# A second buffer for the x tile of the local heads, in an attention and mixture-of-experts kernel

## The chip, the cores and the metric

The kernel runs on one core of a Trainium2 chip. The metric is the time of one execution on the device in microseconds (us); of several runs the median counts. Engines: PE is TensorE (matmul), PEld its weight loads, DVE is VectorE, ACT is ScalarE, POOL is GpSimd, SP is SyncE; the last two issue DMAs here.

## What is computed

Attention over 4 batches, 8 heads, 576 positions and 64 numbers a head, then two feed-forward stages over the 2304 tokens. Four heads look at the 32 positions behind them (local), four at every 32nd position (strided):

```python
rel = pos[:, None] - pos[None, :]
mask_local = (rel >= 0) & (rel < 32)
mask_strided = (rel >= 0) & (pos[None, :] % 32 == pos[:, None] % 32)
attn = softmax(where(mask, q @ k.T / 8, -1e9))     # heads 0-3 local, 4-7 strided
x = (attn @ v) as [2304, 512]
e = argmax(x @ w_gate + modality_bias[modality_id]); x = gate * relu(x @ w1[e]) @ w2[e]
out = elu(x @ w_in) @ w_out
```

## The kernel before

`attention` (line 1072 on) goes over 16 pairs of heads, four for each batch b, in the order 2, 0, 3, 1: pairs 2 and 3 are strided, 0 and 1 local. So pair number n is strided where n is even and local where it is odd. The pairs are pipelined by a loop that is written out by hand; nothing reorders it. Iteration n makes the scores of pair n (`emit_S`: products on TensorE, mask L1274 and maximum L1277 on VectorE, subtraction L1278 on GpSimd), transposes q and k of pair n+1 (`emit_T`), transposes the weights of pair n-1 (`emit_PT`) and multiplies them by v (`emit_PV`), transposes the result of pair n-2 for the router (`emit_X`), then takes the exponential of pair n (`emit_exp`, L1283, on ScalarE between the two copies L1119 of `relay`), and loads q and k of pair n+3 and v of pair n+2 on SyncE's queue. Each engine works through its part in this order.

`emit_PV` ends with VectorE scaling the products, out of PSUM, into an x tile: L1336 for strided pairs, L1365 and L1368 for local ones. Two pairs share one x tile: one tile for the strided heads of a batch (`xs1`) and one for the local heads (`xs0`). The products come out of PSUM banks of the tag P, of which there are four; those of tag T, which the transposes of q and k and the router use, are two.

When the second pair of a tile is done, the stores of the tile to `x_dram` are put on the list `stores`: six for the strided tile (L1344), three for the local one (L1372, L1375). `store_x(3)`, called in `emit_S` right behind the subtraction on GpSimd, issues up to three of them on GpSimd's queue. With this order the six strided stores of a batch are issued three in iteration 4b+4 and three in 4b+5, and the three local ones in iteration 4b+6. In that same iteration `emit_PV` writes the first local pair of batch b+1.

From iteration 9 on a background generator (`early`) puts the routing of batches 0 and 1, the gathers from `x_dram` and the first expert's weights between these steps, one part per step of the loop. After the loop `ffn` runs: matrix products over the experts, then over w_in and w_out, with the rest of the attention (pair 15) threaded in.

Of the kernel before, what the change touches and what calls it, by code (L numbers as in the profile page):

```python
# [8 lines left out]
F32 = mybir.dt.float32  # L9
# [1062 lines left out]
def attention(tc, bg, q, k, v, mod, mbias, wg, x_dram, ident, router, bank):  # L1072
# [8 lines left out]
    xs_p = bctx.enter_context(tc.tile_pool(name="xs", bufs=1, side="right"))  # L1081
# [228 lines left out]
    xs, stores = {}, []  # L1310
# [3 lines left out]
    def emit_PV(n):  # L1314
        b, pr = pairs[n]
        strided = pr >= 2
        key = (b, pr // 2)
        h0 = 2 * (pr % 2)
        if key not in xs:
            sh = [128, 6, 4, D] if strided else [128, 18, D]  # L1320
            xs[key] = xs_p.tile(sh, F32, tag=f"xs{pr // 2}", bufs=1 + pr // 2, name="xs")
        x_sb = xs[key]
        xb = x_dram[b * S:(b + 1) * S]
        if strided:
            pss = [bank("P", "ps_v", 128, 6, D) for w in range(2)]
            for z in range(Z):
                for r in range(2):
                    for x in range(2):
                        for w in range(2):
                            ro = slice(64 * w, 64 * w + N3)  # L1330
                            at = (6 * r + 2 * z + x) * N3
                            nc.tensor.matmul(pss[w][64 * x:64 * x + 64, 2 * z + r], lhsT=pt_s[ro, at:at + 64],
                                             rhs=vs[pr - 2][ro, 3 * x + z, D * r:D * r + D], start=True, stop=True)
            rec = rss.pop(n)
            for w in range(2):
                nc.vector.tensor_tensor(x_sb[:, :, h0 + w], pss[w], rec[:, w].unsqueeze(2).to_broadcast([128, 6, D]), ALU.mult)  # L1336
                bg()
                bg()
            if pr % 2:
                o = xb[:, 4 * D:].rearrange("(j c) d -> j c d", c=32)  # L1340
                for y in range(6):
                    i, x = divmod(y, 2)
                    cnt = min(6, 32 - 6 * y)
                    stores.append(lambda y=y, cnt=cnt, at=64 * x + J * i: nc.gpsimd.dma_start(  # L1344
                        o[:, 6 * y:6 * y + cnt], x_sb[at:at + J, 0:cnt].rearrange("j s h d -> j s (h d)")))
            return
        parts = [(0, TAIL + 1), (TAIL + 1, 9)]
        pss = [bank("P", f"ps_v{r}", 128, j - i, D + 1) for r, (i, j) in enumerate(parts)]
        for r in range(2):
            for s in range(4):  # L1350
                for x in range(2):
                    nc.tensor.matmul(pss[r][64 * x:64 * x + 64, s], lhsT=pt_l[:, parts[r][0] + s, 64 * x:64 * x + 64],
                                     rhs=vl[pr][:, 2 * s + x, r], start=True, stop=True)
        for r in range(2):
            nc.tensor.matmul(pss[0][64 * r:64 * r + 64, TAIL], lhsT=pt_l[:, TAIL, 64 * r:64 * r + 64],
                             rhs=vl[pr][:, 8, r], start=True, stop=True)
        rs = m_p.tile([128, 9], F32, tag="rs", name="rs")
        for ps, (i, j) in zip(pss, parts):
            nc.vector.tensor_scalar(rs[:, i:j], ps[:, :, D], 1e-9, None, ALU.add)
            bg()  # L1360
        nc.vector.reciprocal(rs, rs)
        bg()
        main = x_sb[:, 0:16].rearrange("p (s h) d -> p s h d", h=4)
        for r, (i, j) in enumerate(parts):
            nc.vector.tensor_tensor(main[:, :, h0 + r], pss[r][:, 0:4, 0:D],  # L1365
                                    rs[:, i:i + 4].unsqueeze(2).to_broadcast([128, 4, D]), ALU.mult)
            bg()
        nc.vector.tensor_tensor(x_sb[:, 16 + pr], pss[0][:, TAIL, 0:D], rs[:, TAIL:TAIL + 1].to_broadcast([128, D]), ALU.mult)  # L1368
        rss.pop(n)
        if pr % 2:  # L1370
            o = xb[0:512, 0:4 * D].rearrange("(s p) d -> p s d", p=128)
            stores.append(lambda: nc.gpsimd.dma_start(o, x_sb[:, 0:16].rearrange("p (s h) d -> p s (h d)", h=4)))  # L1372
            e = xb[512:S, 0:4 * D].rearrange("q (i r d) -> r q i d", r=2, d=D)
            for r in range(2):
                stores.append(lambda r=r: nc.gpsimd.dma_start(e[r], x_sb[64 * r:64 * r + 64, 16:18]))  # L1375
# [56 lines left out]
    for n in range(NP):  # L1432
# [14 lines left out]
        if n >= 1:  # L1447
            emit_PV(n - 1)
# [20 lines left out]
        if n + 2 < NP:  # L1469
            load_v(*pairs[n + 2])  # L1470
        bg.flush()
    return SimpleNamespace(PT=emit_PT, PV=emit_PV, X=emit_X, L=emit_L, lg=emit_lg, close_a=actx.close, close_b=bctx.close)


# [26 lines left out]
```

## Time and profile before

| | |
|---|---|
| median of 3 runs | 743.01 us (742.3 to 744.5) |
| the profiled execution | 739.77 us, its span 738.0 us |
| PE busy | 712.9 us, 97% of the span |
| PEld busy | 626.2 us, 85% |
| DVE busy | 553.7 us, 75% |
| ACT busy | 416.5 us, 56% |
| POOL busy | 120.4 us, 16% |
| mean granted TensorE clock | 0.986 of 2.4 GHz |

The numbers come from one profiled execution. Times in the rows are microseconds from the start of the span. The attention loop fills about the first 120 us, the products of the experts and of the last stage the rest. A share of busy time is a mean over both. "Idle before" is how long the engine did nothing ahead of an instruction, and "<-" what ended that; "issue" is what the profile cannot put down to anything. Several instructions of one line in a row stand in one row with their count.

### The profile page before, as it was taken

Reading aid. Unit: us, or ns where it says so; the run is one execution under the profiler, and the core shown is the slowest. Engines: PE = TensorE matmul, PEld = TensorE weight load, DVE = VectorE, ACT = ScalarE, POOL = GpSimd, SP = SyncE. Lnnn points to the kernel's source line nnn. Section 1 sums busy time; section 2 is a strip of 40 time slices with the busy share of each in tenths; the row PEclk is TensorE's granted clock in tenths of the full one; section 3 lists DMA queues with packets and bytes.
Section 4 is the critical chain, followed back from the end, with each engine's and each line's share of the span. In section 5 each row is a group of like instructions: output and inputs, shape, how many; then the busy total and the mean of one; then the engine's idle time right before and its main releaser. Section 6 shows DMA issues by size and latency. Waiting matters only on the chain.

```text
span 738.0 us, 13498 instructions
## 1 busy us (share of the span) xinstructions
PE 712.9 (97%) x5007; PEld 626.2 (85%) x5010; DVE 553.7 (75%) x1066; ACT 416.5 (56%) x761; POOL 120.4 (16%) x182
## 2 busy tenths in 40 slices
PE   8989887999999999999999999999999999999997
PEld 5868676778888888888899989998999989998895
DVE  4758666776879978777788766787787898777763
ACT  5767564325545454545555545585556687556543
POOL 4634363222020110000000000031100003200003
PEclk9999798999999999999999999999999999999999
DMA  9999563356595686564766555255443335543302
GB/s 183 209 234 207 146 194 93 119 172 208 171 291 180 218 280 208 201 218 155 271 233 238 172 186 170 86 171 188 131 167 115 115 117 202 185 153 115 114 1 86
DMA packets 99190, 127.34 MB, mean 173 GB/s; under 512 B 20167, under 2 KB 71911, under 8 KB 99120
## 3 DMA queue, kind: packets, MB, share of 16 engines
q1 hardware_dynamic: 89136, 94.91, 42.7%
q0 software_dynamic: 9984, 31.51, 13.2%
q8 instruction: 41, 0.67, 0.4%
q14 instruction: 29, 0.24, 0.1%
HBM read 100.18 MB, written 26.21 MB: 171 GB/s over the span
## 4 chain that ended last, share of the span: by engine, by line
PE 51%; POOL 1%; issue 0%; POOLq 0%; ACT 0%
PE h_ps L719 25%; PE o_ps L810 9%; PE o_ps L809 9%; PE o_ps L808 9%; POOL out_dram L819 1%; POOLq L1497 0%; ACT y_sb L817 0%; POOLq L819 0%
## 5 line engine op out<-in xcount | busy, mean ns | idle before, releaser
L810 PE MATMUL o_ps<-wh,gl 128*128 128x512 f32 x282 | 111.2, 394 | 0.0
L809 PE MATMUL o_ps<-wl,gh 128*128 128x512 f32 x282 | 111.0, 394 | 0.0
L808 PE MATMUL o_ps<-wh,gh 128*128 128x512 f32 x282 | 110.6, 392 | 0.0
L794 ACT CAST gh<-t 128x384 fp32r<-128x384 f32 x94 | 48.3, 514 | 104.5 <-DVE t L746 101.5
L490 DVE TENSOR_TENSOR wl<-wraw,wh 128x1024 fp32r<-128x1024 f32 x56 | 69.2, 1235 | 33.3 <-ACT wh L489 31.4
L719 PE MATMUL h_ps<-xa,wh 128*128 128x384 f32 x320 | 87.3, 337 | 1.6 <-PEq L756 1.6
L745 DVE SCALAR_TENSOR_TENSOR t<-e,t 128x384 f32<-128x384 f32 x96 | 53.4, 556 | 27.9 <-ACT e L740 25.7
L870 POOL DMA_DIRECT2D wl<-wl_dram x32 | 17.5, 550 | 338.0 <-PE o_ps L810 197.8
L800 DVE TENSOR_TENSOR gl<-t,gh 128x384 fp32r<-128x384 f32 x94 | 52.2, 555 | 18.5 <-ACT gh L794 16.7
L719 PEld LDWEIGHTS h_ps<-xa,wh 128*128 128x128 f32 x320 | 59.2, 188 | 8.1 <-issue 1.9
L719 PE MATMUL h_ps<-xa,wl 128*128 128x384 f32 x192 | 64.6, 336 | 0.0
L810 PEld LDWEIGHTS o_ps<-wh,gl 128*128 128x128 f32 x282 | 53.0, 188 | 12.0
L524 PE MATMUL y_ps<-hh,wh 128*128 128x460 f32 (+1 forms) x160 | 61.4, 384 | 0.0
L526 PE MATMUL y_ps<-hh,wl 128*128 128x460 f32 (+1 forms) x160 | 60.1, 375 | 0.0
L525 PE MATMUL y_ps<-hl,wh 128*128 128x460 f32 (+1 forms) x160 | 60.0, 375 | 0.0
L489 ACT CAST wh<-wraw 128x1024 fp32r<-128x1024 f32 x56 | 58.4, 1042 | 0.0
L809 PEld LDWEIGHTS o_ps<-wl,gh 128*128 128x128 f32 x282 | 53.0, 188 | 6.2
L808 PEld LDWEIGHTS o_ps<-wh,gh 128*128 128x128 f32 x282 | 53.0, 188 | 6.2
L147 ACT ACTIVATE conv<-conv 128x512 f32<-128x512 f32 x32 | 21.7, 679 | 59.2 <-DVE conv L159 59.2
L719 PE MATMUL h_ps<-xb,wh 128*128 128x384 f32 x192 | 54.6, 338 | 0.0
L874 ACT CAST wh<-wraw 128x1024 fp32r<-128x1024 f32 x48 | 50.1, 1043 | 0.0
L719 PE MATMUL h_ps<-xc,wh 128*128 128x384 f32 x192 | 49.3, 338 | 0.0
(271 smaller groups left out, 1608.2 us busy)
## 6 DMA issues: line engine op xcount, KB each, us to landing
wraw<-w_f SPq DMA_DIRECT2D x48, 512.0 KB
wraw<-in_moe_w_dram SPq DMA_DIRECT2D x80, 256.0 KB
wl<-wl_dram POOLq DMA_DIRECT2D x32, 512.0 KB, 4.4
conv<-in_moe_w_in_dram SPq DMA_DIRECT2D x16, 512.0 KB
conv<-in_moe_w_out_dram SPq DMA_DIRECT2D x16, 512.0 KB
w_f<-conv SPq DMA_DIRECT2D x32, 256.0 KB
wl_dram<-wl SPq DMA_DIRECT2D x16, 512.0 KB
qn<-in_q_dram SPq DMA_DIRECT2D x16, 288.0 KB
```

The source lines that it names most:

```text
L489: nc.scalar.copy(WH[i], raw)
L490: nc.vector.tensor_tensor(WL[i], raw, WH[i].bitcast(F32), ALU.subtract)
L524: nc.tensor.matmul(ps, lhsT=a, rhs=hh, start=f == 0, stop=False)
L525: nc.tensor.matmul(ps, lhsT=a, rhs=hl, start=False, stop=False)
L526: nc.tensor.matmul(ps, lhsT=b, rhs=hh, start=False, stop=f == NCH - 1)
L719: mm = lambda x, v, f, l: nc.tensor.matmul(ps, lhsT=x, rhs=v, start=f, stop=l, skip_group_check=on)
L745: nc.vector.scalar_tensor_tensor(t, e, 1.0, t, ALU.add, ALU.mult)
L800: nc.vector.tensor_tensor(gl, t, gh.bitcast(F32), ALU.subtract)
L808: nc.tensor.matmul(ps, lhsT=a, rhs=hi, start=first, stop=False)
L809: nc.tensor.matmul(ps, lhsT=a, rhs=lo, start=False, stop=False)
L810: nc.tensor.matmul(ps, lhsT=b, rhs=hi, start=False, stop=last)
L874: nc.scalar.copy(WH[slots(n)[nm]], wts[n, nm])
```

## The change

One line: the tile of the local heads is taken from two buffers in turn, one for each batch, as that of the strided heads is. Nothing else is touched.

```diff
@@ in emit_PV
         if key not in xs:
             sh = [128, 6, 4, D] if strided else [128, 18, D]
-            xs[key] = xs_p.tile(sh, F32, tag=f"xs{pr // 2}", bufs=1 + pr // 2, name="xs")
+            xs[key] = xs_p.tile(sh, F32, tag=f"xs{pr // 2}", bufs=2, name="xs")
         x_sb = xs[key]
```

## Rows read from the trace of the kernel before

**Rows 1.** Windows: us, busy us (x instructions) of PE, PEld, DVE, ACT, POOL; PEclk, DMA share, GB/s.
```profile
40.00:60.00 20.00, 16.54 (x318) 14.14 (x317) 11.46 (x27) 12.79 (x30) 7.01 (x9) 0.91 1.10 227
...
600.00:738.00 138.00, 132.55 (x653) 118.02 (x651) 100.39 (x192) 80.50 (x149) 19.58 (x24) 1.00 0.35 116
```

**Rows 2.** By line, 0 to 200 us: busy, mean ns, idle before; x stores, issue to landing.
```profile
L1336 DVE TENSOR_TENSOR xs<-ps_v,rec 128x384 f32<-128x384 f32 x16 | 8.3, 553 | 0.7
...
L1365 DVE TENSOR_TENSOR xs<-ps_v,rs 128x256 f32<-128x256 f32 x16 | 6.1, 419 | 14.7 <-DMA x_dram<-xs 14.5
...
DMA to landing us min/median/max: 2.8/4.1/5.6
```

**Rows 3.** Timeline around the first wait: start, us, engine, line, operation, idle before, releaser.
```profile
47.23 1.23 POOL L1375 DMA_DIRECT2D x_dram<-xs  x2
...
47.28 1.06 PE L1267 MATMUL ps_sl<-kt,qt 64*64 64x96 f32 x38
...
52.47 0.76 DVE L1365 TENSOR_TENSOR xs<-ps_v,rs 128x256 f32<-128x256 f32 x2 [5.36 <-DMA x_dram<-xs]
...
53.27 1.11 DVE L1274 TENSOR_TENSOR sm_l<-ps_sl,mask_l 128x480 f32<-128x480 f32 x2
...
53.32 1.31 PE L1332 MATMUL ps_v<-vs,pt_s 54*64 54x64 f32 x48 [2.99 <-issue]
...
54.71 1.05 DVE L1277 TENSOR_REDUCE mx<-sm_l 128x9 f32<-128x864 f32 x1
...
55.71 0.59 ACT L1404 COPY xt<-ps_x 128x512 f32<-128x512 f32 x1 [4.75 <-PE ps_x L1399]
...
55.94 1.63 POOL L1278 TENSOR_TENSOR sm_l<-sm_l,mx 128x864 f32<-128x864 f32 x1 [7.47 <-DVE mx L1277]
...
56.30 0.84 ACT L1119 COPY qr<-qn 96x768 f32<-96x768 f32 x1
...
57.60 0.92 ACT L1283 ACTIVATE sm_l<-sm_l 128x864 f32<-128x864 f32 x1 [0.46 <-POOL sm_l L1278]
```

**Rows 4.** Timeline, the same steps of an iteration without a wait.
```profile
65.51 1.04 PE L1332 MATMUL ps_v<-vs,pt_s 54*64 54x64 f32 x48
...
67.18 0.59 ACT L1404 COPY xt<-ps_x 128x512 f32<-128x512 f32 x1 [0.97 <-PE ps_x L1399]
```

**Rows 5.** Timeline around the second wait.
```profile
77.87 0.47 PE L1228 MATMUL ps_tr<-ident,qn 96*128 96x96 f32 x3 [0.58 <-ACT qt L1232]
...
80.39 0.33 PE L1332 MATMUL ps_v<-vs,pt_s 54*64 54x64 f32 x2
...
81.75 0.42 DVE L1365 TENSOR_TENSOR xs<-ps_v,rs 128x256 f32<-128x256 f32 x1 [6.16 <-DMA x_dram<-xs]
...
87.36 0.92 ACT L1283 ACTIVATE sm_l<-sm_l 128x864 f32<-128x864 f32 x1 [0.62 <-POOL sm_l L1278]
...
87.85 0.56 DVE L1336 TENSOR_TENSOR xs<-ps_v,rec 128x384 f32<-128x384 f32 x1
...
88.34 2.16 PE L1307 MATMUL ps_p<-ident,sm_l 128*96 128x128 f32 x9 [0.23 <-ACT sm_l L1283]
...
93.12 0.23 DVE L1359 TENSOR_SCALAR rs<-ps_v 128x5 f32<-128x5 f32 x2 [0.46 <-PE ps_v L1355]
```

**Rows 6.** Timeline around the third wait.
```profile
114.93 0.76 DVE L1365 TENSOR_TENSOR xs<-ps_v,rs 128x256 f32<-128x256 f32 x2 [3.03 <-DMA x_dram<-xs]
...
116.26 0.87 PE L482 MATMUL x_ps<-ident,xg 128*128 128x128 f32 x2 [3.98 <-DVE xg L471]
```

**Rows 7.** Windows behind the second and the third wait; columns as in rows 1.
```profile
82.00:92.00 10.00, 9.08 (x135) 7.93 (x137) 9.70 (x36) 5.59 (x11) 2.12 (x2) 0.50 0.37 113
...
116.00:122.00 6.00, 5.74 (x65) 4.54 (x66) 5.70 (x12) 2.59 (x5) 1.63 (x1) 0.50 0.01 3
```

**Rows 8.** Timeline of the DMA queue of SP: q loads of pairs 9 and 12.
```profile
43.15 0.32 SPq L1112 DMA_DIRECT2D qn<-in_q_dram  x1
...
57.75 0.32 SPq L1112 DMA_DIRECT2D qn<-in_q_dram  x1
```

## The prediction

> **What bounds the kernel now.** I read the windows first. From 140 us to the end TensorE is busy nearly without a break: I cut that part into eleven windows, and the lowest of them is the last, with 132.55 of 138 us or 96% [rows 1]. Nothing that the change touches runs in that part, so it will take the time it takes; the change can only bring its start forward or push it back. Before that, in the attention stage, no engine is full: from 40 to 60 us TensorE has 16.54 of 20 us, VectorE 11.46, ScalarE 12.79 [rows 1]. That is a loop bound by waits, so I looked for the waits. The view by line shows the two multiplies that write an x tile side by side: L1336, of the strided heads with two buffers, has 0.7 us of idle time before its 16 instructions; L1365, of the local heads with one, has 14.7, and 14.5 of that ended when a store of the x tile to x_dram landed [rows 2]. They are three waits: 5.36, 6.16 and 3.03 us [rows 3, 5, 6], together 14.55, one for each batch after the first. The mechanism stands in the first [rows 3]: GpSimd issues the stores of the old tile at 47.23, in the same iteration in which VectorE comes to the next batch's first multiply (52.47 - 5.36 = 47.11 us). A store takes 4.1 us to land (median, 2.8 to 5.6) [rows 2], so VectorE, which works in order, stands still with masks, maxima and all else queued behind.
>
> **What is removed.** The buffer that batch b+1 takes was last stored by batch b-1, one batch before the stores that are waited for now; two such waits end 81.75 - 52.47 = 29.3 us apart [rows 3, 5], so no landing is near it. The three waits go as such. No instruction and no transfer is added; program order on all engines is unchanged. It costs 4.6 KB of each partition (18 x 64 numbers of 4 bytes). What has to be worked out is what is late next, wait by wait.
>
> **First wait (5.36).** VectorE would multiply at 47.11, be through at 47.11 + (53.27 - 52.47) = 47.91, and find the next scores at 47.28 + 1.06 = 48.34. From the mask to the end of the maximum takes 54.71 + 1.05 - 53.27 = 2.49, so 50.83; GpSimd starts 55.94 - 55.76 = 0.18 later and takes 1.63: 52.64 instead of 57.57 [rows 3]. So far 4.9 us are won. But the exponential behind it is ScalarE's, and ScalarE comes to it only after the copies L1404 and the relay qr. L1404 needs transposes that lie on TensorE behind the products L1332, and these had waited only 2.99 us (for a PSUM bank that the late multiply frees; the row says "issue", but it starts as that multiply ends): they could start at 53.32 - 2.99 = 50.33. In an iteration without a wait L1404 starts 67.18 - 65.51 = 1.67 after L1332 [rows 4]; the relay follows 56.30 - 55.71 = 0.59 later and takes 0.84 [rows 3]. That puts the exponential at 50.33 + 1.67 + 0.59 + 0.84 = 53.43 instead of 57.60: **4.2 us**, and all that follows in this loop (transposes of the weights, products, next multiply) hangs on it. Ends: 2.99, if only TensorE's wait returns, and 5.36.
>
> **Second wait (6.16).** Here VectorE carries the routing work of the first two batches as well: between 81.75 and the wait of 0.46 at 93.12 it has no idle row, so it is the bound of the next two iterations [rows 5]. Its multiply would run at 75.59 and the next product's scaling at 87.85 - 6.16 = 81.69. That needs L1332, whose first two had already run at 80.39 before the bank stopped the rest: 80.39 + 1.04 = 81.43, in time. ScalarE's exponential would come at 80.39 + 1.67 + 0.59 + 0.84 = 83.49 instead of 87.36: 3.9 us. Two things help it on. One of the two banks with the tag T holds the rank table until L305, which stands behind the waiting multiply; TensorE's transposes of the next pair then share one bank and wait 0.58 us, twice (at 77.87 and two transposes later) [rows 5]: 1.2 us. And the nine transposes of L1307 took 2.16 us at half the clock: at the full level 1.1 less. 3.9 + 1.2 + 1.1 = 6.2, about what VectorE itself gains. I take **5.8**; ends 3.9 and 6.16.
>
> **Third wait (3.03).** The multiply runs at 111.90; behind it stand two scalings of gathered rows, for which TensorE waited 3.98 us at 116.26 [rows 6]. After it VectorE is busy 5.70 of the 6 us to 122 [rows 7], so it is the bound and the whole 3.03 comes through; its 0.30 of idle time there is what a faster TensorE could add. I take **3.2**; ends 3.03 and 3.33.
>
> **The clock.** After the second and the third wait the granted clock is 0.50, the lower of its two levels, for all of 82 to 92 and 116 to 122 us [rows 7]; ahead of the third TensorE had stood idle for 3.98 us [rows 6]. Such gaps go with the waits, so I count on full clock there; what it is worth is in the terms above. The Trainium skill, "TensorE: Matmul & The Clock Gate", section "HAM oscillation — how this bites in real kernels", describes just this: work that waits for a DMA lets the clock fall, and the next piece starts slow. The trace agrees; by that rule all time at half clock returns, which is the second rival.
>
> **Sum.** 4.2 + 5.8 + 3.2 = 13.2 us of the profiled execution's 739.77 (its span 738.0 and 1.8 around it). That one was a little faster than the median of the runs, 743.01; scaled by 743.01 / 739.77 = 1.0044 it is 13.3: **729.8 us**. With the lower ends, 2.99 + 3.9 + 3.03 = 9.9, it is 733.1; with the upper, 5.36 + 6.16 + 3.33 = 14.85, it is 728.1.
>
> **Rivals.**
> *The loads become the bound.* From 40 to 60 us the DMA engines have a share of 1.10, no free time [rows 1], and while VectorE stood still the loads went on. SyncE issues the loads of q for pairs 9 and 12 at 43.15 and 57.75, 4.87 us a pair [rows 8]. The four iterations from the first multiply, now ready at 47.11, to the second, ready at 75.59 - 4.2 = 71.4, would take 6.1 us each, so the loads still keep ahead; and pair 9's, wanted by the relay at 52.59, have 9.4 us, where the slowest x store took 5.6 [rows 2]. If they were the bound all the same, the first term would be lost (later the share is far lower: 0.37 from 82 to 92 [rows 7]): 9.0 us, 734.0. The Trainium skill, "DMA: Bandwidth & Descriptors", section "Issuing engines are not separate DMA queues", speaks for this one: transfers issued by different engines run on the same 16 DMA engines and interleave, so x stores, now never waited for, still take time from the loads. The share of 1.10 agrees with that; the issue times say that there is room.
> *All waits and all half clock return.* TensorE would have to be the bound in the third place: half of its 5.74 busy us from 116 to 122, 2.9 [rows 7]. 5.36 + 6.16 + 3.03 + 2.9 = 17.4: 725.5. Against it: VectorE is as busy there.
> *The wait stays*, because the multiply waits for something else at that place, or the tile's memory is not new: 743.0. Against it: L1336 is the same construction and has no such wait [rows 2].
> *Slower, by the clock at the seam.* The change moves TensorE's gaps. Should one now fall just ahead of 122 us, the products that fill TensorE to the end would start at half clock, where each us costs half a us. To end over 0.3% (2.2 us) slower it would have to eat 13.3 + 2.2 = 15.5 us, some 31 us at half clock; the longest such stretch here is about 10 [rows 7], so 5 us. One such stretch would leave 734.8, still faster; it decides from three times that length on, and four of them, 40 us, would give 749.7.
>
> **How the numbers follow.** Forecast 0.78, loads 0.10, everything returns 0.07, the wait stays 0.03, slower 0.02. The range takes the forecast's ends and the loads' case; at the lower end I add what the best run lies under the median (743.01 - 742.3 = 0.7): 727.4 to 734.0. A measurement here tells about 0.3% from no change (2.2 us). Faster: 0.95, same 0.03, slower 0.02.
>
> **What would show it.** Right: no idle time before L1365 that a store ended; the exponential of the first place some 4 us earlier, of the second 10, TensorE's unbroken stretch 13 earlier, and the rest of the span equally long; a granted clock near 1.00 between 45 and 125 us. Wrong: relays or transposes that wait for q or k (loads); L1359 or L1336 waiting for TensorE for several us more than now (the chain over ScalarE returns less than I count); a window at 0.50 behind 125 us.

## The result, and the profile after

| | before | after |
|---|---|---|
| median | 743.56 us (742.3 to 744.5, 4 runs) | 734.32 us (732.95 to 735.55, 4 runs) |
| the profiled execution | 739.77 us, span 738.0 | 735.35 us, span 733.6 |
| mean granted clock | 0.986 | 0.984 |

Ratio 0.9876, 95% interval 0.9849 to 0.9904: faster by 9.2 us. The forecast was 729.8, a ratio of 0.9822, with a range up to 734.0. The direction held, the size did not.

The waits that the change aims at are gone. By line, VectorE from 0 to 200 us (busy, mean ns, idle before and what ended it); these answer to [rows 2], where L1365 had 14.7 us:

```profile
L1274 DVE TENSOR_TENSOR sm_l<-ps_sl,mask_l 128x480 f32<-128x480 f32 (+1 forms) x16 | 9.0, 602 | 8.0 <-remote 4.4 <-PE ps_sl L1267 3.5
L1336 DVE TENSOR_TENSOR xs<-ps_v,rec 128x384 f32<-128x384 f32 x16 | 8.3, 553 | 0.8
...
L1365 DVE TENSOR_TENSOR xs<-ps_v,rs 128x256 f32<-128x256 f32 x16 | 6.1, 419 | 0.2
L1359 DVE TENSOR_SCALAR rs<-ps_v 128x5 f32<-128x5 f32 (+1 forms) x16 | 1.9, 158 | 9.3 <-PE ps_v L1355 9.3
L1425 DVE TENSOR_TENSOR lg<-ps_g,bias 128x32 f32<-128x32 f32 (+1 forms) x4 | 0.8, 196 | 5.7 <-PE ps_g L1424 5.7
```

How far ahead of before the changed kernel is, is read by setting the same instruction of both beside each other. Timeline after, at the places of [rows 3, 5]: the exponential and the next scaling behind the first wait, then those behind the second.

```profile
46.87 0.76 DVE L1365 TENSOR_TENSOR xs<-ps_v,rs 128x256 f32<-128x256 f32 x2
...
52.86 0.93 ACT L1283 ACTIVATE sm_l<-sm_l 128x864 f32<-128x864 f32 x1
...
70.84 0.42 DVE L1365 TENSOR_TENSOR xs<-ps_v,rs 128x256 f32<-128x256 f32 x1
...
76.92 0.93 ACT L1283 ACTIVATE sm_l<-sm_l 128x864 f32<-128x864 f32 x1
...
83.20 0.23 DVE L1359 TENSOR_SCALAR rs<-ps_v 128x5 f32<-128x5 f32 x2 [1.34 <-PE ps_v L1355]
```

57.60 - 52.86 = 4.7 us ahead behind the first wait, 93.12 - 83.20 = 9.9 behind the second: the first two terms came as forecast (4.2, and 4.2 + 5.8 = 10.0). Then comes something that the rows of before do not have. The same timeline goes on:

```profile
85.57 1.07 POOL L467 DMA_INDIRECT xg<-x_dram,idx  x1 [0.61 <-DVE gates L413]
...
89.49 0.95 POOL L467 DMA_INDIRECT xg<-x_dram,idx  x1 [0.30 <-issue]
89.98 1.12 DVE L1274 TENSOR_TENSOR sm_l<-ps_sl,mask_l 128x480 f32<-128x480 f32 x2 [4.43 <-remote]
91.44 0.76 ACT L1232 COPY qt<-ps_tr 128x324 f32<-128x324 f32 x2 [5.69 <-remote]
91.92 0.47 PE L1228 MATMUL ps_tr<-ident,kn 96*128 96x96 f32 x3 [4.25 <-ACT qt L1232]
...
95.68 2.48 PE L1413 MATMUL ps_l<-xt,wgp 128*32 128x288 f32 x16
...
100.01 0.19 DVE L1425 TENSOR_TENSOR lg<-ps_g,bias 128x32 f32<-128x32 f32 x1 [4.19 <-PE ps_g L1424]
...
109.24 0.74 DVE L1365 TENSOR_TENSOR xs<-ps_v,rs 128x256 f32<-128x256 f32 x2
```

While GpSimd issues the four gathers of the first expert's rows (L467), VectorE, ScalarE and TensorE all stand still for 4 to 6 us; "remote" means that the profile names no instruction as the releaser. TensorE's records of the products and transposes waited for begin at 84.80 to 86.83, but its semaphore events (the updates of a counter by which the other engines learn that TensorE is done) are recorded at 89.89 to 91.53, 2.2 to 3.8 us after any of its instructions had ended by the records. Then TensorE runs at the lower clock from 92.50 to 106.16: L1413 takes 2.48 us, where it takes 1.66 at the full level (in e5, below), and L1425 waits 4.19. Windows (columns as in rows 1):

```profile
84.00:92.00 8.00, 3.75 (x65) 3.31 (x65) 3.07 (x11) 2.08 (x5) 4.91 (x6) 0.90 1.07 314
92.00:106.00 14.00, 14.00 (x167) 11.45 (x169) 6.85 (x12) 9.11 (x20) 4.46 (x5) 0.52 0.33 97
...
345.00:349.00 4.00, 4.00 (x14) 3.96 (x15) 3.29 (x6) 2.54 (x6) 0.00 (x0) 0.57 0.91 321
```

VectorE before, at places that are compared here and below:

```profile
61.84 0.23 DVE L1359 TENSOR_SCALAR rs<-ps_v 128x5 f32<-128x5 f32 x2 [0.99 <-PE ps_v L1355]
...
101.51 0.19 DVE L1425 TENSOR_TENSOR lg<-ps_g,bias 128x32 f32<-128x32 f32 x1 [1.47 <-PE ps_g L1424]
105.26 1.22 DVE L490 TENSOR_TENSOR wl<-wraw,wh 128x1024 fp32r<-128x1024 f32 x1 [3.56 <-ACT wh L489]
```

L1425 stands at 101.51 in before, so of 9.9 us ahead 1.5 are left. The third L1365 runs at 109.24 without a wait, 114.93 - 109.24 = 5.7 ahead: the gain of the third wait is in that, and 1.9 from a wait of L490 for weights, 3.56 in before and 1.67 now. At the L1365 after that (129.14 in before, 122.97 now) it is 6.2. The end is 738.0 - 733.6 = 4.4 us earlier, so some 1.8 us are lost far behind; a stretch at half clock at 345 us, 3.4 us long, is new there (1.00 in before), which at half speed would be 1.7.

So two questions: does the change make the stop at the gathers, or did the profiled execution of before just not have it? And what makes the stop? In what follows, the kernels of one group ran on one chip, together with runs of the kernel before: e1 to e4 on chip A (before 742.83), e5 to e8 on B (744.79), e9 to e12 on C (740.63), e13 to e15 on D (743.38), e16 to e18 on E (744.39).

### The profile page after: what moved, and what is told of

The parts are those of the page before. It is cut to its first block, busy times and chain, and to the rows that moved or that the text cites. A ratio compares the mean times of both kernels' runs of the same rounds, so it can differ in the third digit from the quotient of the medians.

```text
span 733.6 us, 13503 instructions
## 1 busy us (share of the span) xinstructions
PE 713.0 (97%) x5007; PEld 626.4 (85%) x5010; DVE 554.4 (76%) x1066; ACT 418.2 (57%) x761; POOL 120.4 (16%) x182
## 4 chain that ended last, share of the span: by engine, by line
PE 51%; POOL 1%; issue 0%; POOLq 0%; ACT 0%
PE h_ps L719 25%; PE o_ps L810 9%; PE o_ps L809 9%; PE o_ps L808 9%; POOL out_dram L819 1%; POOLq L1497 0%; ACT y_sb L817 0%; POOLq L819 0%
## 5 line engine op out<-in xcount | busy, mean ns | idle before, releaser
L490 DVE TENSOR_TENSOR wl<-wraw,wh 128x1024 fp32r<-128x1024 f32 x56 | 68.6, 1224 | 31.4 <-ACT wh L489 29.5
```

The costliest lines, as they stand in the source:

```text
L490: nc.vector.tensor_tensor(WL[i], raw, WH[i].bitcast(F32), ALU.subtract)
```

## Experiments: the change in three parts

e1 repeats the changed kernel. e2 to e4 remove one wait each: the second buffer serves one batch alone.

```diff
-            xs[key] = xs_p.tile(sh, F32, tag=f"xs{pr // 2}", bufs=2, name="xs")
+            # e2: b > 0     e3: b > 1     e4: b > 2
+            xs[key] = xs_p.tile(sh, F32, tag="xs1" if strided else f"xs0{b > 0}", bufs=2 if strided else 1, name="xs")
```

> The changed kernel once more. Theory A (the 5 us stop of VectorE and ScalarE at 85.6 to 91.4 us and the half clock from 92.5 to 106 us follow from the change): they stand there again, VectorE idle over 3 us between the routing table and the mask of the next local pair, the clock near 0.5 behind it, and the time is again 733 to 736 us. Theory B (an accident of single executions, which comes at any place and in the kernel before too): no stop at that place, the granted clock stays near 1.0 from 85 to 106 us, and the span is 8 us shorter than 733.6, some 725 us.

> The second buffer is taken from batch 1 on and kept: only the first of the three waits goes. Theory A and B alike: the maximum of pair 9 comes 4.2 to 4.7 us earlier than in the kernel before and the two other waits stand as they were (6.2 and 3.0 us); the time is 743.5 - 4.5 = 739 us. If it is the density of work after the first wait that brings the new stop, it shows here too, and the time is 743 us or so.

> The second buffer is taken from batch 2 on: only the second wait, the one before the routing work, goes. Theory A: the stop behind the routing table is there (3 us or more of VectorE idle) with half clock behind it, and of the 5.8 us at most 1 us is left: 742.5 us. Theory B: no such stop, 743.5 - 5.8 = 737.7 us.

> The second buffer is taken for batch 3 alone: only the third wait goes. Both theories: no stop at the routing table that the kernel before has not; 3.0 to 3.3 us are saved, 740.3 us, and the half clock from 116 to 122 us goes.

| chip A | median | ratio to before, interval | gain | term of the forecast |
|---|---|---|---|---|
| e1 all three | 733.76 | 0.9851 (0.9811 to 0.989) | 9.1 | 13.3 |
| e2 first alone | 739.77 | 0.9953 (0.9922 to 0.9984) | 3.1 | 4.2 |
| e3 second alone | 739.73 | 0.9958 (0.9936 to 0.9979) | 3.1 | 5.8 |
| e4 third alone | 740.79 | 0.9967 (0.9945 to 0.999) | 2.0 | 3.2 |

Each wait is worth something alone, 8.2 us together. The timelines of VectorE say where the rest goes. e2:

```profile
57.03 0.23 DVE L1359 TENSOR_SCALAR rs<-ps_v 128x5 f32<-128x5 f32 x2 [1.43 <-PE ps_v L1355]
...
78.56 0.42 DVE L1365 TENSOR_TENSOR xs<-ps_v,rs 128x256 f32<-128x256 f32 x1 [7.88 <-DMA x_dram<-xs]
...
98.77 1.02 DVE L1336 TENSOR_TENSOR xs<-ps_v,rec 128x384 f32<-128x384 f32 x2 [3.02 <-PE ps_v L1332]
...
103.30 0.19 DVE L1425 TENSOR_TENSOR lg<-ps_g,bias 128x32 f32<-128x32 f32 x1 [3.50 <-PE ps_g L1424]
```

4.8 us are won at the first wait (61.84 in before against 57.03); the second wait grows from 6.16 to 7.88, so 3.2 reach the second multiply (81.75 - 78.56). Then L1336 and L1425 at the gathers wait 3.02 and 3.50 us, and L1425 stands 1.8 us behind the profiled execution of before. e3 shows the same at its place:

```profile
88.14 0.23 DVE L1359 TENSOR_SCALAR rs<-ps_v 128x5 f32<-128x5 f32 x2 [1.52 <-PE ps_v L1355]
...
105.14 0.19 DVE L1425 TENSOR_TENSOR lg<-ps_g,bias 128x32 f32<-128x32 f32 x1 [4.63 <-PE ps_g L1424]
...
116.09 0.76 DVE L1365 TENSOR_TENSOR xs<-ps_v,rs 128x256 f32<-128x256 f32 x2 [1.86 <-DMA x_dram<-xs]
```

5.0 us ahead at L1359, 3.6 behind at L1425, and a part of that given back by the third wait, which shrinks from 3.03 to 1.86 because the multiply comes later. The stop is at the gathers in e1 and e4 as well (L1425 waits 3.69 and 4.03). e4:

```profile
110.34 0.19 DVE L1425 TENSOR_TENSOR lg<-ps_g,bias 128x32 f32<-128x32 f32 x1 [4.03 <-PE ps_g L1424]
```

In e4 no wait ahead of the gathers was touched, so the stop does not need one removed. And the profiled execution of before, 739.77, lies below every one of the 24 timed runs of before on this chip (lowest 741.47). This speaks for theory B; the next experiment asks directly.

## Experiments: what makes the stop

e5 is the kernel before, profiled again. e6 issues the gathers two steps later; e7 and e8 replace them by plain loads of as many bytes, after and before: the rows come in their order and are not those that the router chose, so both leave out the choice of rows for the first job.

```diff
 # e6, in early()
-        for c in range(4):
-            gather(jobs[0], c)
-            yield STEP if c == 3 else None
         fetch_to(1)
         yield STEP
         yield STEP
+        for c in range(4):
+            gather(jobs[0], c)
+            yield STEP if c == 3 else None
 # e7, e8, in gather()
-        nc.gpsimd.indirect_dma_start(t, None, rows, bass.IndirectOffsetOnAxis(job.idx[:, c:c + 1], 0))
+        nc.gpsimd.dma_start(t, rows[128 * c:128 * c + 128]) if job is jobs[0] else nc.gpsimd.indirect_dma_start(t, None, rows, bass.IndirectOffsetOnAxis(job.idx[:, c:c + 1], 0))
```

> The kernel before, profiled once more. Theory A (the stop of some 3 to 6 us at the place of the four gathers L467, and the half clock behind it, come from the change): the profile is as in [rows 1 to 7], 739 to 740 us, no stop over 1 us at the gathers. Theory B (the stop belongs to that place in most executions of either kernel, and the profiled execution on which the prediction rests was one without it): VectorE or ScalarE stand still for 2 to 5 us while GpSimd issues the gathers, the score multiply L1425 behind them waits over 3 us instead of 1.5, and the execution takes 742 to 744 us.

> The changed kernel with the four gathers of the routed rows issued two steps of the background work later, behind the weight loads that had followed them; the same work in all. If the gathers make the stop, it goes with them: VectorE and ScalarE run through the place at 85 to 91 us and stand still where GpSimd now issues L467, some 3 to 4 us later. If something else at that place makes it (x stores, the loads of weights or of v, the iteration itself), it stays at 85 to 91. The total: 732 to 736 us by either.

> The changed kernel with the four gathers of the first job as plain loads of as many bytes (4 times 128 rows of 2 KB, the rows in their order and not those that the router chose, so the outputs of the first job's tokens are others). If the gathers by index make the stop and with it the half clock, both go: 729 to 731 us, no stop over 1 us between 83 and 92 us, granted clock near 1.00 there. If the amount of traffic or another thing at the place makes it: the stop stays and the time with it, 733 to 736.

> The kernel before with the same plain loads in the place of the first job's four gathers. If the gathers by index make the stop in this kernel too (theory B): 738 to 740.5, and the change is then worth about 9 to 10 us beside it, since its three terms are not touched. If they make it only after the change (theory A): 742 to 744, no different from the kernel before, and the change is worth some 13 us without the gathers.

e5 took 742.72 us, and the kernel before has a stop at its gathers as well. Timeline of e5:

```profile
96.42 1.07 POOL L467 DMA_INDIRECT xg<-x_dram,idx  x1 [0.30 <-issue]
97.77 1.18 DVE L1274 TENSOR_TENSOR sm_l<-ps_sl,mask_l 128x480 f32<-128x480 f32 x2 [1.87 <-PE ps_tr L1229]
...
98.50 0.43 ACT L1232 COPY qt<-ps_tr 128x324 f32<-128x324 f32 x1 [2.41 <-PE ps_p L1291]
...
102.03 0.64 PE L1332 MATMUL ps_v<-vs,pt_s 54*64 54x64 f32 x24 [0.38 <-issue]
...
103.45 1.66 PE L1413 MATMUL ps_l<-xt,wgp 128*32 128x288 f32 x16
106.26 0.19 DVE L1425 TENSOR_TENSOR lg<-ps_g,bias 128x32 f32<-128x32 f32 x1 [1.89 <-PE ps_g L1424]
```

It is smaller than after (1.87 and 2.41 us), and L1425 does not wait the 3 us that theory B asked for; but between the second multiply (82.10 against 81.75) and L1425 (106.26 against 101.51) this execution falls from 0.4 to 4.8 us behind the one of the prediction. So the kernel before has the stop too, as in e4, and the execution of the prediction lacked it: theory A is out.

| | median | ratio to before on that chip | |
|---|---|---|---|
| e6 after, late gathers (B) | 728.44 | 0.9793 (0.9739 to 0.9846) | |
| e7 after, plain loads (B) | 727.16 | 0.9781 (0.9722 to 0.9839) | |
| e8 before, plain loads (B) | 740.71 | 0.9953 (0.9923 to 0.9982) | e8 - e7 = 13.5 us |

With plain loads the stop is gone in both kernels, and the change is worth 13.5 us, nearly the forecast 13.3; by the two intervals this difference is uncertain by some 5 us. In e6 it is small: at the gathers' new place (from 92.40) TensorE's events are 0.38 to 0.48 us late, and ScalarE waits 1.31 us there (L1238). The same place in e7:

```profile
85.59 1.12 DVE L1274 TENSOR_TENSOR sm_l<-ps_sl,mask_l 128x480 f32<-128x480 f32 x2
85.64 2.20 POOL L467 DMA_DIRECT2D xg<-x_dram  x4
85.98 0.76 ACT L1232 COPY qt<-ps_tr 128x324 f32<-128x324 f32 x2 [0.55 <-PE ps_tr L1229]
...
91.92 0.19 DVE L1425 TENSOR_TENSOR lg<-ps_g,bias 128x32 f32<-128x32 f32 x1 [0.50 <-PE ps_g L1424]
```

and its windows:

```profile
84.00:92.00 8.00, 7.98 (x164) 6.30 (x165) 6.94 (x18) 5.83 (x15) 7.27 (x11) 1.00 1.02 296
```

The DMA engines are as full as in the changed kernel (1.02 against 1.07; 296 against 314 GB/s), so the amount of traffic alone does not make the stop. No semaphore event of TensorE is late there.

## Experiments: the place, the load beside it, or the chip

e9 takes another suspect away, the load of v for the last pair, which moves in rows of 256 bytes while the gathers are issued. e10 spreads the gathers over four steps. e11 and e12 put the late gathers into both kernels.

```diff
 # e9
-        if n + 2 < NP:
+        if n + 2 < NP - 1:
             load_v(*pairs[n + 2])
 # and in early(), behind the fourth weight load
-        fetch_to(3)
+        fetch_to(3); bg.last_v()          # load_v(*pairs[NP - 1])
 # e10
         for c in range(4):
             gather(jobs[0], c)
-            yield STEP if c == 3 else None
-        fetch_to(1)
-        yield STEP
-        yield STEP
+            if c == 1: fetch_to(1)
+            yield STEP if c < 3 else None
```

> The changed kernel with the load of v for the last pair (L1135, L1136, which SyncE issues at 83.95 to 86.3 us there and whose rows of 256 bytes are under way while GpSimd issues the gathers) put behind the fourth weight load, some 15 us later. If the stop needs both the gathers by index and these small rows beside them, it goes: no wait over 1 us at 84 to 92 us, 728 to 730 us. If the gathers by index stop the engines whatever is loaded beside them: stop as in the changed kernel, 733 to 735.

> The changed kernel with the four gathers issued one in each step of the background work, the first at the same place and the last three steps later. If a single gather by index costs the others its share, the stop comes in four pieces of about 1 us, 733 to 735 us. If only the row of four in sequence (some 5 us of GpSimd) makes it, or the place where they lie: 728 to 730.

> The kernel of the late gathers with the second buffer, once more, beside the following one. If that position costs less because little else hangs on it: 728 to 729 us again, and 13 to 14 us under the following kernel, as in the forecast for the change alone (13.3).

> The kernel before with the gathers at the late position, without the second buffer. If the gathers cost the kernel before some 3 to 4 us at their old place: 739 to 741 us, and the change is worth 11 to 13 here. If the late position is of use only with the second buffer: 742 to 744.

On chip C: e9 726.61, e10 728.42 (724.75 to 735.42), e11 727.75, e12 740.54 with before at 740.63 (ratio 0.9997, 0.9972 to 1.0022). Between e11 and e12 the change is worth 740.54 - 727.75 = 12.8 us. Alone these times would have read as three remedies that work. But the kernel before is itself faster here than on the other chips, e12 gains nothing, and none of these four profiles has a late semaphore event, though in e9 the gathers by index stand where they stood. Timeline of e9:

```profile
86.28 1.12 DVE L1274 TENSOR_TENSOR sm_l<-ps_sl,mask_l 128x480 f32<-128x480 f32 x2
86.64 1.07 POOL L467 DMA_INDIRECT xg<-x_dram,idx  x1 [0.30 <-issue]
...
90.55 0.95 POOL L467 DMA_INDIRECT xg<-x_dram,idx  x1 [0.30 <-issue]
92.62 0.19 DVE L1425 TENSOR_TENSOR lg<-ps_g,bias 128x32 f32<-128x32 f32 x1 [1.40 <-PE ps_g L1424]
```

So the chip had to be ruled out, with the changed kernel and both remedies side by side (e13 is the changed kernel, e14 has the edit of e6, e15 that of e9).

> The changed kernel beside the two that follow, on one chip with them. If the stop belongs to the gathers at this place wherever the kernel runs: 733 to 735 us, VectorE's wait of over 2 us at 85 to 92 us. If it belongs to the chip (the profiles of the two kernels e11 and e12 have no late semaphore update at the gathers, those of e1 to e6 have): on a chip without it 727 to 730, with a gain of 12 to 13.5 us on the kernel before, as forecast; on a chip with it 733 to 735.

> The changed kernel with the four gathers two steps later (as e6 and e11). If the gathers' place makes the stop: 727 to 729, 5 to 6 us under e13. If the chip makes it and this chip has none: the same as e13 within 1 us; if this chip has it and the place is without effect: as e13 too, at 733 to 735.

> The changed kernel with the last load of v behind the fourth weight load (as e9). If the stop needs the small rows of v beside the gathers: 726 to 729 and no wait over 1 us at 84 to 92 us, whatever e13 shows. If the gathers alone make it, on a chip that has it: 733 to 735, as e13.

On chip D the late events are there, and the three agree: 731.45 (ratio 0.9846, 0.9821 to 0.9872), 730.65 (0.982, 0.9792 to 0.9849), 730.92 (0.9836, 0.9813 to 0.9859). Neither the place of the gathers nor the v load is worth anything that can be measured. All three wait where their gathers are: 1.49 us at L1274 in e14, 1.88 at L1336 and 2.57 at L1425 in e15, and in e13:

```profile
89.08 1.20 DVE L1274 TENSOR_TENSOR sm_l<-ps_sl,mask_l 128x480 f32<-128x480 f32 x2 [3.67 <-PE ps_p L1291]
...
91.21 0.76 ACT L1232 COPY qt<-ps_tr 128x324 f32<-128x324 f32 x2 [5.60 <-remote]
...
95.41 1.58 PE L1413 MATMUL ps_l<-xt,wgp 128*32 128x288 f32 x16
...
98.16 0.19 DVE L1425 TENSOR_TENSOR lg<-ps_g,bias 128x32 f32<-128x32 f32 x1 [3.06 <-PE ps_g L1424]
```

The stop is as large as in the first profile after (3.67 and 5.60 against 4.43 and 5.69), but the half clock behind it lasts from 92.55 to 95.96 only, L1413 takes 1.58, and the span is 729.7, 3.9 us shorter. The reading of e6 (the late place cures it) is not confirmed: here the late place gains 0.8 us, within noise, and on chip B, where e5 has the stop, the changed kernel was not run beside e6.

Last, the plain loads again with the changed kernel beside them.

> The changed kernel once more, beside the two with plain loads. On a chip where the records show late semaphore updates of TensorE at the gathers: 731 to 735 us, a stop of 2 to 5 us there. On one without: 726 to 729, a gain of about 13, as forecast, and the second iteration of the gathers without a wait over 1 us.

> The changed kernel with the first job's four gathers as plain loads of as many bytes (the outputs of that job's tokens are others), as e7. If the gathers by index are what stops the engines where they are stopped: 726 to 728 on any chip, so 4 to 7 us under e16 on a chip with late updates and within 1.5 us of it on one without. If not: as e16 on either.

> The kernel before with the same plain loads, as e8. Without the gathers' stop the change should be worth what the forecast says, 12.5 to 14 us: 739.5 to 741 beside 726 to 728 of e17. If the third wait or the clock eats a part of the gain also without the stop, the two stand less than 11 us apart.

| chip E | median | ratio to before (744.39) |
|---|---|---|
| e16 after | 730.29 (728.73 to 737.4) | 0.9823 (0.9787 to 0.9859) |
| e17 after, plain loads | 727.13 | 0.9779 (0.974 to 0.9818) |
| e18 before, plain loads | 738.64 | 0.9918 (0.9895 to 0.994) |

e16 has the stop once more, now in small pieces: TensorE's L1332 comes in three with 0.25 to 0.42 us between, and behind them L1425 waits longest.

```profile
90.96 0.99 PE L1332 MATMUL ps_v<-vs,pt_s 54*64 54x64 f32 x24 [0.42 <-issue]
...
91.97 1.02 DVE L1336 TENSOR_TENSOR xs<-ps_v,rec 128x384 f32<-128x384 f32 x2 [2.55 <-PE ps_v L1332]
93.33 2.48 PE L1413 MATMUL ps_l<-xt,wgp 128*32 128x288 f32 x16
97.66 0.19 DVE L1425 TENSOR_TENSOR lg<-ps_g,bias 128x32 f32<-128x32 f32 x1 [4.67 <-PE ps_g L1424]
```

In e17 that row is

```profile
92.52 0.19 DVE L1425 TENSOR_TENSOR lg<-ps_g,bias 128x32 f32<-128x32 f32 x1 [0.49 <-PE ps_g L1424]
...
101.62 0.73 DVE L1365 TENSOR_TENSOR xs<-ps_v,rs 128x256 f32<-128x256 f32 x2
```

So the stop goes with the gathers by index. With plain loads it is absent in four profiles on two chips, and between 75 and 130 us no event of TensorE is over 0.12 us late in them, as none is on chip C. The other 12 profiles with gathers by index all have events at the first four gathers that are 0.25 us late or more: at most 0.3 in the profiled execution of before, 0.5 in e6, 4.0 in e3. But the index alone does not make it: the later gathers of the same line, from 125 to 264 us, bring no event over 0.3 us late in any profile, though the DMA share is 0.96 from 249 to 255 us in the first profile after.

By the medians the gathers by index cost the kernel before 744.39 - 738.64 = 5.8 us here and 4.1 on chip B, both clear of noise. They cost the changed kernel 730.29 - 727.13 = 3.2, which is not: the two intervals overlap. The change is worth 14.1 us with them and 11.5 without, each uncertain by some 3 us, so no difference between the two is shown. Of the versions that gather the rows that the router chose, none was shown faster than the changed kernel on one chip with it.

## Why the prediction was right and where it was wrong

**First and second wait.** Right, in mechanism and size: 4.7 us at the exponential (4.2), 9.9 us at L1359 (10.0). The chain over L1332, L1404 and the relay sets the first, as said: L1332 starts at once in the new timeline, at 49.99, and the exponential follows 52.86 - 49.99 = 2.9 us later, against 57.60 - 53.32 = 4.3 [rows 3].

**Third wait.** The wait is gone, but not as a term to be added: VectorE came to it behind a stop, and a later arrival had shortened it already (1.86 in e3). Without the stop it returns: in e17 L1365 runs at 101.62, 13.3 us ahead of before, where L1425 was 9.0 ahead; 3.0 of these 4.3 us are the wait.

**The clock.** "I count on full clock there" failed. Removing the three DMA waits did not remove TensorE's gaps, because another wait, not in the rows, lay between the second and the third. In the changed kernel the clock was at half from 92.50 to 106.16. Without the stop it nearly holds: from 80 to 100 us 1.00 in e7 and 0.91 in e17, from 100 to 120 us 0.91 in both, where the changed kernel has 0.73 and 0.85. Short stretches stay even so, each 3.4 us long: 82.26 to 85.67 in the changed kernel, ahead of the gathers, and 109.44 to 112.86 in e17. The Trainium skill, "TensorE: Matmul & The Clock Gate", section "HAM oscillation — how this bites in real kernels", ties the lower clock to work that waits for a DMA. The traces agree in the main for the three waits: from 40 to 125 us before has 20.5 us at half clock, e17 6.8 and e7 3.4. Behind the gathers it came after a gap for which the profile names no DMA.

**The sum.** This is the step that failed: the stop at the gathers was no term of it. I took the profiled execution as one "a little faster than the median" and scaled it by 1.0044, as if the 3.24 us between (743.01 - 739.77) were spread over the whole. In e5, the other profile of that kernel, they arise at one place: it loses 4.4 us between the second multiply and L1425 and is 3.0 longer at the end. The profiled execution was one all but without the stop. Against executions like itself the sum is right: 739.77 - 13.2 = 726.6 us, and the changed kernel with plain loads takes 727.16 and 727.13 (e7, e17), its profiled executions 725.27 and 727.37. What was to be forecast was the median with the stop. Subtracting from the median of before leaves the 3.24 us of before in the sum, and what the stop costs the changed kernel beyond that was no term at all (the factor itself is worth 0.1 us). In the first profile after, 9.9 us ahead at L1359 became 1.5 at L1425. By the medians the price is 734.32 - 727.1 = 7 us in the first runs (across chips) and 3.2 on chip E. Some 7 in the changed kernel against 3.24 in before leave the forecast 4 us too low; it was 734.32 - 729.8 = 4.5 too low. Why the stop cost the changed kernel more in the first runs is not shown.

**How large the gain is.** The four measurements of the change are 9.2, 9.1 (chip A), 11.9 (D) and 14.1 us (E). The forecast ratio of 0.9822 lies outside the interval of the first (from 0.9849 on) and within those of the other three, at the very edge in D. Without the stop the removed waits are worth 13.5 us (B, plain loads), 11.5 (E, plain loads) and 12.8 (C, late gathers in both), which agrees with the forecast within noise. With the gathers in place a group of runs shows between 9 and 14.

**The rivals.** *Loads* gave 734.0, which is nearly the measured time, for another reason: it wanted the first term lost, and that came in full. The sharing behind it (the Trainium skill, "DMA: Bandwidth & Descriptors", section "Issuing engines are not separate DMA queues", by which transfers of different engines interleave on the same DMA engines) cost nothing here: the share is 1.06 from 40 to 60 us after, 1.10 before [rows 1], and no relay waits for a load there. *All waits and all half clock return* (725.5) is out: a part of the half clock stayed. *The wait stays* and *slower* are out. A window at 0.50 behind 125 us was named as a sign of being wrong; a short one came (345 us, 0.57), in the first profile after and not in e1, e13 and e16.

**What stays open.** By which path these gathers hold up the others: the runs show late semaphore events of TensorE where the first four are issued, on four of five chips, and none with plain loads. But a plain load differs in more than the index (GpSimd is through with four after 2.20 us instead of some 4.9), and one cause was not separated from the other. Nor is it settled why chip C shows none, why the later gathers bring none, why the stop was so small in the profiled execution of before (its 739.77 us lies within the runs of chip C, 738.91 to 745.37, but its events are 0.3 us late, where those of chip C are not), and why the half clock behind the stop lasts 3.4 us in one execution (e13) and 13.7 in another. That the size of the gain follows from this length is argued from two profiles (e13 and the first after), not shown.

## What to carry to other kernels

Before you add terms to one profiled execution, ask where the difference between it and the median lies: an execution below all timed runs may lack a stall that the others have, and no factor stands for that. Profile the kernel before a second time when a forecast rests on a few microseconds. When remedies are compared, put the kernel without them beside them on the same chip: three of them seemed to work on chip C, and the two that were run again on D were worth nothing that could be measured.

## What the runs showed that I had not expected

Gathers by index (4 of 128 rows of 2 KB, GpSimd 0.95 to 1.07 us each) went with stops of up to 5.7 us on engines that do not wait for their data, and with semaphore events of TensorE up to 4.0 us late (e3), on four of five chips and at the first four gathers only; plain loads of the same bytes did not (L1274 waits 0.86 us or less there). They cost the kernel before 4.1 us (chip B) and 5.8 (E), more than the forecast gave the third wait (3.2).
